# Two chained MoE layers: layer 2 of the first two blocks moved directly behind their layer 1

## The chip, the cores and the metric

The kernel runs on one core of one Trainium2 chip. The metric is the device time of one execution in microseconds. Of the kernel before three timed runs gave 1136.51, 1136.9 and 1136.9 us (median 1136.9). One further execution was profiled and took 1136.92 us.

## The reference

The input is convolved along the sequence with seven softmax-weighted taps per head (causal, zeros ahead of the start). Two dense layers follow, each in the form g(x W_in) W_out, over 8192 tokens of 192 channels with 2048 hidden columns:

```python
w = softmax(weight)                      # 8 heads x 7 taps
x = sum_k w[head, k] * x_pad[s + k]      # 2 x 4096 tokens x 192 channels
h = x @ moe_w_in                         # 192 -> 2048
g = where(h >= 1, h, where(h <= -1, 0, (h + 1) ** 2 / 4))
x = g @ moe_w_out                        # 2048 -> 192
h = x @ moe2_w_in
g = h / (1 + exp(-1.702 * h))
out = g @ moe2_w_out
```

## The kernel before

Channels lie on partitions, tokens on the free axis. The tokens are cut into 16 blocks of 512, the hidden columns of each layer into 16 slices of 128. The 192 channels of a block are a tile of 128 (a) and one of 64 (b). Every operand of a matmul is split into a high part, cast to fp32r on ACT, and a low part, the rest, subtracted on DVE (`split`, L72), and products of parts are summed in PSUM.

A unit is one slice of one layer of one block. For a unit `gemm1` makes 128 hidden rows in one of four PSUM banks (tile h), `act_a` applies the activation (layer 1: relu and square on ACT and a min on DVE, L272 to L274; layer 2: one ACT op, L276), `act_b` splits the result into ghi and glo, and `gemm2`, four units later (LAG), adds its product to the block's two accumulators. When the last slice has been added, `finish` reads the accumulators: for layer 1 into the input of layer 2 (tiles xah, xal and xb, by way of s), for layer 2 into the output.

A phase is one layer of one block: (1, 0) is layer 1 of block 0. The list `phases` (L211) and the list `units` (L219) set the order of all units by hand: blocks 0 and 1 take turns in layer 1, then block 2 goes through layer 1, then blocks 0 and 1 take turns in layer 2, and from there layer 1 of block i and layer 2 of block i - 1 alternate.

The first 32 units (WHOLE) run as whole steps: five matmuls of gemm1 and five of gemm2 over all 128 partitions (L250, L315). From there on `both` runs pairs of two units as pieces over 64 partitions, two at a time in the two halves of the array (L361). In a pair the odd unit reads the lower channels from a second copy of xb whose halves are exchanged, xc; two DMAs on SP make it (`swap_halves`, L177 to L179).

What isn't a step of a unit is put beside one: `at(step, op)` (L404) appends an operation to that step's list, and `beside` issues the list behind the step's own work. All engines take their instructions in the order in which they were issued. Three things lie there:

- Weight tiles arrive as 64-bit floats in two words. `convert_at` (L470) fetches a tile three steps ahead and turns it into a high and a low part in four steps: `begin` (an ACT op into wa, L117, and a shift on DVE into wd, L118), `join` (DVE, L122), `high_part` (a cast on ACT into wt, L127), `low_part` (two subtractions on DVE into wt, L131 and L132). A unit's gemm1 reads the low part first.
- The convolution of blocks 2j and 2j + 1 (`conv_at`, L424): seven taps on DVE for the upper channels of block 2j (cva), `put_a`, seven for the lower channels of both (cvb), and `put_b`, which splits them into xb and issues the two DMAs for xc. They begin 22 steps ahead of block 2j's layer 1, one a step. The upper channels of block 2j + 1 follow from 16 steps ahead of its own layer 1.
- The later parts of `finish` for layer 1: adding the two halves of the lower channels one step later, splitting them two steps later.

In the steady part the numbers of the first units of layer 1 of blocks 4, 6, ... 14 are 112, 176, ... 432.

Of the kernel before, what the change touches and what calls it, by code (L numbers as in the profile page):

```python
# [20 lines left out]
def kernel(  # L21
# [21 lines left out]
    nc = tc.nc  # L43
    NBLK, D, _ = out.shape
    K = taps_in.shape[2]
    NF, _, WC = w1.shape
    DB = D - P
    B = P // DB
    PAD = K - 1
    H = P // 2  # L50
    LAG = 4
    CH = 4
# [11 lines left out]
    ps = ctx.enter_context(tc.tile_pool(name="ps", bufs=1, space=bass.MemoryType.PSUM))  # L64
# [7 lines left out]
    def split(src, hi, lo):  # L72
        nc.scalar.copy(hi, src)  # L73
        nc.vector.tensor_sub(lo, src, f32(hi))  # L74
# [64 lines left out]
    def new_xs():  # L139
        return [xs_p.tile([P, T], F32R, tag=t, name=t) for t in ("xah", "xal", "xb", "xc")]  # L140
# [7 lines left out]
    def conv_taps(part, t, c):  # L148
        def tap(k):
            w, x = taps[:, part, k : k + 1], t[:, k : k + T]  # L150
            if k == 0:
                return lambda: nc.vector.tensor_scalar_mul(c, x, w)
            return lambda: nc.vector.scalar_tensor_tensor(c, x, w, c, op0=ALU.mult, op1=ALU.add)  # L153

        return [tap(k) for k in range(K)]
# [18 lines left out]
    def put_a(i, c):  # L174
        split(c, *x1[i][:2])
# [14 lines left out]
    def conv_ops(j):  # L190

        ta, tb = xt[0, B * j], xt[1, j]
        ca = cv_p.tile([P, T], F32, tag="cva", name="cva")
        cb = cv_p.tile([P, T], F32, tag="cvb", name="cvb", bufs=1)
        x1[B * j] = new_xs()
        ops = conv_taps(0, ta, ca) + [lambda: put_a(B * j, ca)]
        ops += conv_taps(1, tb, cb) + [lambda: put_b(B * j, cb)]
        st = {}

        def begin():  # L200
            st["c"] = cv_p.tile([P, T], F32, tag="cva", name="cva")
            x1[B * j + 1] = new_xs()
            st["ops"] = conv_taps(0, xt[0, B * j + 1], st["c"])
            put_b(B * j + 1, cb)

        ops.append(begin)
        ops += [lambda: st["ops"].pop(0)() for _ in range(K)] + [lambda: put_a(B * j + 1, st["c"])]
        return ops


    phases = [(1, 0), (1, 1), (1, 2), (2, 0), (2, 1)]  # L211
    for i in range(3, NBLK):
        phases += [(1, i), (2, i - 1)]
    phases += [(2, NBLK - 1)]

    def in_turn(*ps):
        return [(p, c + f) for c in range(0, NF, CH) for p in ps for f in range(CH)]

    units = in_turn(0, 1) + in_turn(2) + in_turn(3, 4)  # L219
    units += [(p, f) for p in range(5, len(phases)) for f in range(NF)]  # L220
    unit_at = {u: k for k, u in enumerate(units)}

    hid, act, halves, accs = {}, {}, {}, {}
# [145 lines left out]
    def finish(p, step):  # L369
        n, i = phases[p]  # L370
        acc_a, acc_b = accs.pop(p)
        if n == 1:
            ah, al, b, c = x2[i] = new_xs()
            s = cv_p.tile([P, T], F32, tag="cva", name="s")
            nc.scalar.copy(s[0:DB], acc_b[DB:P])
            split(acc_a, ah, al)
            at(step + 1, lambda: nc.vector.tensor_add(s[0:DB], acc_b[0:DB], s[0:DB]))  # L377

            def put():
                split(s[0:DB], b[0:DB], b[DB:P])  # L380
                if phases.index((2, i)) * NF >= WHOLE:
                    swap_halves(c, b)

            at(step + 2, put)
        else:
            o = o_p.tile([P, 2, T], F32, tag="o", name="o")
            nc.scalar.copy(o[0:DB, 1], acc_b[DB:P])
            nc.vector.tensor_add(o[0:DB, 1], acc_b[0:DB], o[0:DB, 1])
            if p < len(phases) - 1:
                nc.scalar.copy(o[:, 0], acc_a)  # L390
                nc.sync.dma_start(out[i, 0:P], o[:, 0])
                nc.sync.dma_start(out[i, P:D], o[0:DB, 1])
            else:
                near, far = slice(0, T // 2), slice(T // 2, T)
                nc.scalar.copy(o[:, 0, near], acc_a[:, near])
                nc.sync.dma_start(out[i, 0:P, near], o[:, 0, near])
                nc.scalar.copy(o[:, 0, far], acc_a[:, far])
                nc.scalar.dma_start(out[i, 0:P, far], o[:, 0, far])
                nc.sync.dma_start(out[i, P:D], o[0:DB, 1])
# [4 lines left out]
    def at(step, op):  # L404
        plan.setdefault(max(step, 0), []).append(op)

    def fetch_w(n, f):
        raw[n, f] = weight_load(n, f)
# [11 lines left out]
    def fetch_x(*which):  # L420
        for part, i in which:
            xt[part, i] = x_load(part, i)

    def conv_at(j):  # L424
        first, second = (unit_at[phases.index((1, B * j + k)), 0] for k in range(B))
        ops = []
        at(first - 30, lambda: fetch_x((0, B * j), (1, j), (0, B * j + 1)))
        at(first - 22, lambda: ops.extend(conv_ops(j)))
        for k in range(2 * (K + 1)):
            at(first - 22 + k, lambda: ops.pop(0)())  # L430
        for k in range(K + 2):
            at(second - 16 + k, lambda: ops.pop(0)())

    with tc.manual_schedule():
        nc.sync.dma_start(taps, taps_in)
        fetch_x((0, 0), (1, 0))
        fetch_w(1, 0)
        fetch_w(1, 1)
        fetch_x((0, 1))
        fetch_w(1, 2)  # L440

        make_identity(nc, ident)
        warm_up()
        softmax_taps()

        nc.scalar.activation(const.tile([P, 1], F32, name="table"), ident[:, 0:1], AF.Gelu_apprx_sigmoid)
        for i in range(B):
            x1[i] = new_xs()
        ca = cv_p.tile([P, T], F32, tag="cva", name="cva")
        cb_ps, ca_ps = bank(3, "cb_ps"), bank(2, "ca_ps")  # L450
        a0 = conv_taps(0, xt[0, 0], ca)
        b_ops = conv_on_pe(1, xt[1, 0], cb_ps, ident, nc.scalar.mul)
        a1 = conv_on_pe(0, xt[0, 1], ca_ps, ident, nc.gpsimd.tensor_scalar_mul)
        for op in b_ops:
            op()

        ws = [weight_ops(1, f, raw.pop((1, f))) for f in range(CH - 1)]
        order = a0[0:3] + ws[0][0:1] + a0[3:5] + ws[0][1:3] + a0[5:7] + ws[0][3:4] + ws[1][0:1]
        order += [lambda: put_a(0, ca)] + ws[1][1:2] + [lambda: put_b(0, cb_ps)] + ws[1][2:] + ws[2]
        for op in order:  # L460
            op()
        fetch_w(1, 3)
        for k, op in enumerate(weights_at(1, 3)):
            at(k // 2, op)
        for k, op in enumerate(a1):
            at((k + 2) // 3, op)
        at(1, lambda: put_b(1, cb_ps))
        at(2, lambda: put_a(1, ca_ps))

        def convert_at(n, f, steps):  # L470
            at(steps[0] - 3, lambda: fetch_w(n, f))
            for step, op in zip(steps, weights_at(n, f)):
                at(step, op)

        for f in range(CH, NF):
            s = f - 2 if f < 2 * CH else 2 * f - 2 * CH - 1
            convert_at(1, f, range(s, s + 4))
        for f in range(NF):
            s = 2 * NF - 2 + 4 * f if f < CH else 3 * NF - 2 + 2 * (f - CH)
            convert_at(2, f, range(s, s + 4))  # L480
        for j in range(1, NBLK // B):
            conv_at(j)

        def beside(step):
            for op in plan.get(step, []):
                op()

        def finish_if_last(u, step):
            if 0 <= u < len(units) and units[u][1] == NF - 1:
                finish(units[u][0], step)  # L490


        for step in range(WHOLE):
            gemm1(step)
            act_a(step)
            if step >= 1:
                act_b(step - 1)
            if step >= LAG:
                gemm2(step - LAG)
            finish_if_last(step - LAG - 1, step)  # L500
            beside(step)


        act_b(WHOLE - 1)
        for u in range(WHOLE, len(units) + LAG + 4, 2):
            v = u - LAG
            if u == WHOLE:
                finish_if_last(v - 1, u)
                gemm1(u)
                gemm2(v)  # L510
                gemm1(u + 1)
                gemm2(v + 1)
            elif u < len(units):
                both(u, v)
            elif v < len(units):
                gemm2(v)
                gemm2(v + 1)
            if u < len(units):
                for op in (act_a, act_b):
                    op(u)  # L520
                    op(u + 1)
            finish_if_last(v + 1, u + 1)
            for step in (u, u + 1):
                beside(step)
# [55 lines left out]
```

## Time and profile before

| | |
|---|---|
| median of the timed runs | 1136.9 us |
| profiled execution | 1136.92 us |
| its span, first to last instruction | 1135.1 us |
| busy in the span: PE, ACT, DVE | 1126.0, 824.1, 715.2 us |
| granted clock of TensorE | 0.9 or more of full speed in every slice |
| DMA | 36.69 MB, mean 32 GB/s |

All times in the rows count from the start of the span. Matmuls are pipelined and their ends are modelled, so a PE that is busy in the table need not be at its peak; idle time of PE, where it is shown in brackets behind a row with the instruction that ended it, is time in which no matmul ran. The DVE and ACT columns matter only where PE waits for them. In the span's 40 slices of 28.4 us DVE shows 7 to 9 tenths in the first five and 4 to 7 in the others, up to the last few.

### The profile page before, as it was taken

What the parts mean: (1) busy time and instruction counts of PE and PEld (TensorE: products, weight loads), DVE (VectorE), ACT (ScalarE), POOL (GpSimd) and SP (SyncE); (2) the same over time, 40 slices, a digit from 0 to 9 for tenths busy, and PEclk for the clock granted to TensorE, in tenths of its full rate; (3) what the DMA queues carried; (4) which work ended last, traced back from release to release, by engine and by line L of the source; (5) the groups of instructions that cost most, each with busy time, mean ns of one, the idle gap of its engine ahead of it and who ended that gap; (6) DMA issues with size and microseconds to landing.
All of it is one profiled execution on the core that took longest, in us unless ns stands there. A gap on an engine that the chain in (4) does not pass through costs nothing.

```text
span 1135.1 us, 23124 instructions
## 1 busy us (share of the span) xinstructions
PE 1126.0 (99%) x9468; PEld 1009.6 (89%) x9468; DVE 715.2 (63%) x1152; ACT 824.1 (73%) x1468; POOL 7.6 (1%) x13
## 2 busy tenths in 40 slices
PE   9999999999999999999999999999999999999998
PEld 5878889999999999999999999999999999999997
DVE  7997866674657756476564756647566575655532
ACT  7988976867758677686876758677586776868654
POOL 2000000000000000000000000000000000000000
PEclk9999999999999999999999999999999999999999
DMA  5312330100001000010000000010000100000000
GB/s 176 125 28 65 111 97 27 57 10 25 11 10 43 18 17 10 11 43 20 15 19 15 30 19 15 20 43 1 20 15 20 43 1 20 15 20 15 11 15 15
DMA packets 16841, 36.69 MB, mean 32 GB/s; under 512 B 2528, under 2 KB 2784, under 8 KB 16736
## 3 DMA queue, kind: packets, MB, share of 16 engines
q1 hardware_dynamic: 16592, 35.09, 10.5%
q8 instruction: 75, 1.23, 0.5%
q14 instruction: 30, 0.25, 0.1%
q10 hardware_dynamic: 144, 0.13, 0.0%
HBM read 21.05 MB, written 6.29 MB: 24 GB/s over the span
## 4 chain that ended last, share of the span: by engine, by line
PE 93%; DVE 3%; ACT 2%; issue 1%; POOL 0%; POOLq 0%; DVEq 0%
PE acc L361 47%; PE h L361 42%; PE acc L315 1%; PE h L250 1%; DVE glo L74 1%; DVE a L274 1%; ACT a L273 1%; ACT a L272 1%; PE cb_ps L170 1%; PE ca_ps L170 1%; DVE wd L122 0%; PE warm L161 0%; ACT ghi L73 0%; ACT wa L117 0%; ACT wt L127 0%
## 5 line engine op out<-in xcount | busy, mean ns | idle before, releaser
L361 PE MATMUL acc<-ghi,wt 64*128 64x512 f32 x2868 | 869.0, 386 | 0.3 <-ACT ghi L73 0.3
L361 PE MATMUL h<-xah,wt 64*128 64x512 f32 x1912 | 738.2, 386 | 0.0
L361 PE MATMUL acc<-glo,wt 64*128 64x512 f32 x1912 | 706.1, 386 | 0.1
L361 PEld LDWEIGHTS acc<-ghi,wt 64*128 64x128 f32 x2868 | 489.6, 184 | 29.8 <-ACT ghi L73 0.7
L74 DVE TENSOR_TENSOR glo<-a,ghi 128x512 fp32r<-128x512 f32 x512 | 341.6, 688 | 228.8 <-ACT ghi L73 218.6
L361 PEld LDWEIGHTS acc<-glo,wt 64*128 64x128 f32 x1912 | 351.8, 184 | 20.1 <-DVE glo L74 0.8
L361 PEld LDWEIGHTS h<-xah,wt 64*128 64x128 f32 x1912 | 351.8, 184 | 19.8 <-issue 0.4
L361 PE MATMUL h<-xal,wt 64*128 64x512 f32 x956 | 369.2, 386 | 0.0
L73 ACT CAST ghi<-a 128x512 fp32r<-128x512 f32 x512 | 301.3, 614 | 28.3 <-DVE a L274 28.1
L274 DVE SCALAR_TENSOR_TENSOR a<-h,a 128x512 f32<-128x512 f32 x256 | 176.9, 691 | 161.3 <-ACT a L273 161.2
L276 ACT ACTIVATE a<-h 128x512 f32<-128x512 f32 x256 | 151.3, 596 | 155.0 <-PE h L361 147.1
L361 PE MATMUL h<-xb,wt 64*128 64x512 f32 x717 | 238.8, 386 | 0.0
L361 PE MATMUL h<-xc,wt 64*128 64x512 f32 x717 | 238.7, 386 | 0.0
L272 ACT ACTIVATE a<-h 128x512 f32<-128x512 f32 x256 | 151.0, 590 | 53.6 <-PE h L361 53.3
L361 PEld LDWEIGHTS h<-xal,wt 64*128 64x128 f32 x956 | 175.9, 184 | 9.7
L273 ACT ACTIVATE a<-a 128x512 f32<-128x512 f32 x256 | 161.8, 632 | 8.2
L361 PEld LDWEIGHTS h<-xc,wt 64*128 64x128 f32 x717 | 131.9, 184 | 9.6
L361 PEld LDWEIGHTS h<-xb,wt 64*128 64x128 f32 x717 | 131.9, 184 | 5.0
L153 DVE SCALAR_TENSOR_TENSOR cva<-xt,taps,cva 128x512 f32<-128x512 f32 x90 | 67.3, 748 | 1.2
L153 DVE SCALAR_TENSOR_TENSOR cvb<-xt,taps,cvb 128x512 f32<-128x512 f32 x42 | 31.3, 746 | 0.4
L250 PE MATMUL h<-xah,wt 128*128 128x512 f32 x68 | 28.3, 417 | 2.6 <-DVE wt L131 2.6
L73 ACT CAST xb<-s 64x512 fp32r<-64x512 f32 x16 | 9.9, 621 | 28.2 <-DVE s L377 28.2
(61 smaller groups left out, 417.8 us busy)
## 6 DMA issues: line engine op xcount, KB each, us to landing
raw<-in_w_dram SPq DMA_DIRECT2D x32, 448.0 KB, 3.5
xc<-xb SPq DMA_DIRECT2D x46, 128.0 KB, 2.2
xt<-in_xa_dram SPq DMA_DIRECT2D x16, 259.0 KB, 3.5
out_dram<-o SPq DMA_DIRECT2D x15, 256.0 KB, 2.0
out_dram<-o SPq DMA_DIRECT2D x17, 128.0 KB, 2.3
xt<-in_xb_dram SPq DMA_DIRECT2D x8, 259.0 KB, 3.2
xb<-xc SPq DMA_DIRECT2D x14, 128.0 KB, 2.2
out_dram<-o ACTq DMA_DIRECT2D x1, 128.0 KB, 1.8
```

What stands on the lines that cost most here:

```text
L73: nc.scalar.copy(hi, src)
L74: nc.vector.tensor_sub(lo, src, f32(hi))
L153: return lambda: nc.vector.scalar_tensor_tensor(c, x, w, c, op0=ALU.mult, op1=ALU.add)
L170: return lambda: nc.tensor.matmul(c, d[:, k], t[:, k : k + T], start=k == 0, stop=k == K - 1)
L250: nc.tensor.matmul(h, w, r, start=j == 0, stop=j == len(prods) - 1)
L272: nc.scalar.activation(a, h, AF.Relu, bias=0.5, scale=0.5)
L273: nc.scalar.activation(a, a, AF.Square)
L274: nc.vector.scalar_tensor_tensor(a, h, 1.0, a, op0=ALU.max, op1=ALU.min)
L276: nc.scalar.activation(a, h, AF.Gelu_apprx_sigmoid)
L315: nc.tensor.matmul(acc, w, r, start=id(acc) in fresh, stop=last and ends[id(acc)] == k)
L361: mm = nc.tensor.matmul(banks[n], w, r, start=n in fresh, stop=ends.get(n) == k)
```

## The change

`phases` and `units` put layer 2 of blocks 0 and 1 directly behind their layer 1, in turns of 8 units, with block 2's layer 1 behind both (its first unit is 64 instead of 32). In layer 1 the turns are no longer all 4 long: block 0 ends at unit 25 instead of 27. Layer 2's weight tiles are converted from step 22 on, in place of step 30. The steps that follow the evacuation of blocks 0 and 1 (`soon`) come one or two steps sooner, and in whole steps `finish` itself comes one step sooner. The convolutions of even blocks start 18 steps ahead of their layer 1, and their fetches 28. WHOLE is unchanged.

```diff
--- before.py
+++ after.py
@@ -208,16 +208,22 @@
         return ops
 
 
-    phases = [(1, 0), (1, 1), (1, 2), (2, 0), (2, 1)]
+    phases = [(1, 0), (1, 1), (2, 0), (2, 1), (1, 2)]
     for i in range(3, NBLK):
         phases += [(1, i), (2, i - 1)]
     phases += [(2, NBLK - 1)]
 
-    def in_turn(*ps):
-        return [(p, c + f) for c in range(0, NF, CH) for p in ps for f in range(CH)]
-
-    units = in_turn(0, 1) + in_turn(2) + in_turn(3, 4)
-    units += [(p, f) for p in range(5, len(phases)) for f in range(NF)]
+    def in_turn(*runs):
+        made, us = {}, []
+        for p, n in runs:
+            f = made.get(p, 0)
+            us += [(p, f + k) for k in range(n)]
+            made[p] = f + n
+        return us
+
+    units = in_turn((0, 4), (1, 4), (0, 4), (1, 4), (0, 4), (1, 2), (0, 4), (1, 6))
+    units += in_turn((2, 8), (3, 8), (2, 8), (3, 8))
+    units += [(p, f) for p in range(4, len(phases)) for f in range(NF)]
     unit_at = {u: k for k, u in enumerate(units)}
 
     hid, act, halves, accs = {}, {}, {}, {}
@@ -374,14 +380,15 @@
             s = cv_p.tile([P, T], F32, tag="cva", name="s")
             nc.scalar.copy(s[0:DB], acc_b[DB:P])
             split(acc_a, ah, al)
-            at(step + 1, lambda: nc.vector.tensor_add(s[0:DB], acc_b[0:DB], s[0:DB]))
+            soon = i < B
+            at(step + (not soon), lambda: nc.vector.tensor_add(s[0:DB], acc_b[0:DB], s[0:DB]))
 
             def put():
                 split(s[0:DB], b[0:DB], b[DB:P])
                 if phases.index((2, i)) * NF >= WHOLE:
                     swap_halves(c, b)
 
-            at(step + 2, put)
+            at(step + (1 - i if soon else 2), put)
         else:
             o = o_p.tile([P, 2, T], F32, tag="o", name="o")
             nc.scalar.copy(o[0:DB, 1], acc_b[DB:P])
@@ -424,10 +431,10 @@
     def conv_at(j):
         first, second = (unit_at[phases.index((1, B * j + k)), 0] for k in range(B))
         ops = []
-        at(first - 30, lambda: fetch_x((0, B * j), (1, j), (0, B * j + 1)))
-        at(first - 22, lambda: ops.extend(conv_ops(j)))
+        at(first - 28, lambda: fetch_x((0, B * j), (1, j), (0, B * j + 1)))
+        at(first - 18, lambda: ops.extend(conv_ops(j)))
         for k in range(2 * (K + 1)):
-            at(first - 22 + k, lambda: ops.pop(0)())
+            at(first - 18 + k, lambda: ops.pop(0)())
         for k in range(K + 2):
             at(second - 16 + k, lambda: ops.pop(0)())
 
@@ -476,7 +483,7 @@
             s = f - 2 if f < 2 * CH else 2 * f - 2 * CH - 1
             convert_at(1, f, range(s, s + 4))
         for f in range(NF):
-            s = 2 * NF - 2 + 4 * f if f < CH else 3 * NF - 2 + 2 * (f - CH)
+            s = (22, 24, 25, 27, 28, 30, 31, 32)[f] if f < NF // 2 else 36 + (3 * f - 3 * NF // 2) // 2
             convert_at(2, f, range(s, s + 4))
         for j in range(1, NBLK // B):
             conv_at(j)
@@ -497,7 +504,7 @@
                 act_b(step - 1)
             if step >= LAG:
                 gemm2(step - LAG)
-            finish_if_last(step - LAG - 1, step)
+            finish_if_last(step - LAG, step)
             beside(step)
 
 
@@ -505,7 +512,6 @@
         for u in range(WHOLE, len(units) + LAG + 4, 2):
             v = u - LAG
             if u == WHOLE:
-                finish_if_last(v - 1, u)
                 gemm1(u)
                 gemm2(v)
                 gemm1(u + 1)
```

What this moves on the engines, at three places. First DVE near units 24 and 25, the end of layer 1's weight conversion. The number behind a tile's name is that of its allocation, but for h, where the number right behind the letter is the unit (h24 is unit 24); a row with `a<-h` is the min of that unit. Before:

```order
L274 SCALAR_TENSOR_TENSOR a_807<-h24_801,a_807 128x512
L74 TENSOR_TENSOR glo_812<-a_786,ghi_811 128x512
L131 TENSOR_TENSOR wt1_88<-wd_753,wt1_88 128x384
L132 TENSOR_TENSOR wt1_88<-wd_753,wt1_88 128x64
L153 SCALAR_TENSOR_TENSOR cvb_477<-xt_272,taps_85,cvb_477 128x512
L274 SCALAR_TENSOR_TENSOR a_829<-h25_823,a_829 128x512
L74 TENSOR_TENSOR glo_834<-a_807,ghi_833 128x512
L74 TENSOR_TENSOR xb_480<-cvb_477,xb_480 64x512
L274 SCALAR_TENSOR_TENSOR a_852<-h26_846,a_852 128x512
L74 TENSOR_TENSOR glo_857<-a_829,ghi_856 128x512
```

After:

```order
L280 SCALAR_TENSOR_TENSOR a_791<-h24_785,a_791 128x512
L74 TENSOR_TENSOR glo_796<-a_770,ghi_795 128x512
L131 TENSOR_TENSOR wt1_88<-wd_731,wt1_88 128x384
L132 TENSOR_TENSOR wt1_88<-wd_731,wt1_88 128x64
L118 TENSOR_SCALAR wd_808<-raw_734 128x448
L280 SCALAR_TENSOR_TENSOR a_819<-h25_813,a_819 128x512
L74 TENSOR_TENSOR glo_824<-a_791,ghi_823 128x512
L131 TENSOR_TENSOR wt2_89<-wd_759,wt2_89 128x384
L132 TENSOR_TENSOR wt2_89<-wd_759,wt2_89 128x64
L122 SCALAR_TENSOR_TENSOR wd_808<-wa_807,wd_808 128x448
```

In both, the low part of layer 1's last tile (L131 and L132 into wt1, from wd_753 before and wd_731 after) stands behind the min of unit 24 and the subtraction of unit 23. Before, a tap of the convolution and later the split of cvb follow; now layer 2's tiles do. The first unit that reads the tile is 27 before and 25 after.

Second ACT where block 0's layer 1 is evacuated (rows with s and xah), up to the cast of its lower channels (xb) or, before, to where that cast isn't reached yet. Before:

```order
L375 COPY s_977<-acc1_0_310 64x512
L73 CAST xah_973<-acc0_0_309 128x512
L272 ACTIVATE a_1003<-h32_981 128x512
L273 ACTIVATE a_1003<-a_1003 128x512
L272 ACTIVATE a_1007<-h33_992 128x512
L273 ACTIVATE a_1007<-a_1007 128x512
L73 CAST ghi_1011<-a_1003 128x512
```

After:

```order
L381 COPY s_941<-acc1_0_304 64x512
L73 CAST xah_937<-acc0_0_303 128x512
L127 CAST wt2_89<-wd_885 128x448
L278 ACTIVATE a_956<-h30_950 128x512
L279 ACTIVATE a_956<-a_956 128x512
L73 CAST ghi_960<-a_924 128x512
L127 CAST wt2_89<-wd_913 128x448
L117 ACTIVATE wa_972<-raw_888 128x448
L73 CAST xb_939<-s_941 64x512
L278 ACTIVATE a_986<-h31_980 128x512
```

Before, the units behind the evacuation are those of block 2's layer 1 (h32 and h33), and the cast of xb comes behind two more of them. Now it stands between units 30 and 31, with two copies and a first op of layer 2's tiles ahead of it, and unit 32 is the first that reads xb.

Third ACT ahead of layer 1 of block 4, whose first unit is 112, in the steady part; a row `xb<-cvb` is the cast of the convolution's lower channels. Before:

```order
L276 ACTIVATE a_3321<-h104_3277 128x512
L276 ACTIVATE a_3323<-h105_3278 128x512
L73 CAST ghi_3325<-a_3321 128x512
L73 CAST ghi_3329<-a_3323 128x512
L73 CAST xb_2903<-cvb_2900 64x512
L276 ACTIVATE a_3382<-h106_3338 128x512
L276 ACTIVATE a_3384<-h107_3339 128x512
L73 CAST ghi_3386<-a_3382 128x512
L73 CAST ghi_3390<-a_3384 128x512
L276 ACTIVATE a_3438<-h108_3394 128x512
L276 ACTIVATE a_3440<-h109_3395 128x512
```

After:

```order
L73 CAST ghi_3445<-a_3441 128x512
L73 CAST ghi_3449<-a_3443 128x512
L73 CAST xb_3031<-cvb_3028 64x512
L282 ACTIVATE a_3502<-h110_3458 128x512
L282 ACTIVATE a_3504<-h111_3459 128x512
L73 CAST ghi_3506<-a_3502 128x512
L73 CAST ghi_3510<-a_3504 128x512
L278 ACTIVATE a_3558<-h112_3514 128x512
L279 ACTIVATE a_3558<-a_3558 128x512
L278 ACTIVATE a_3562<-h113_3515 128x512
L279 ACTIVATE a_3562<-a_3562 128x512
```

The cast stood behind unit 105, with three pairs between it and unit 112. It now stands behind unit 109, with one pair between them. DVE's subtraction and the two DMAs for xc follow it in both.

## Rows read from the trace of the kernel before

**Rows 1.** Windows by stage: stretch, its length, busy us (instructions) of each engine.

```profile
core 0: us, PE busy (x) PEld busy (x) DVE busy (x) ACT busy (x) POOL busy (x), PEclk, DMA share, GB/s
...
44.40:79.30 34.90, 32.27 (x142) 25.87 (x140) 34.84 (x70) 30.45 (x56) 0.00 (x0) 1.00 0.13 40
...
118.20:1121.60 1003.40, 1003.40 (x8856) 914.95 (x8854) 609.72 (x952) 718.31 (x1273) 0.00 (x0) 1.00 0.08 24
...
```

**Rows 2.** Timeline of PE, pairs: start, duration, instruction, idle before and releaser.

```profile
112.75 0.39 PE L361 MATMUL h<-xah,wt 64*128 64x512 f32 x1
113.44 0.50 PE L361 MATMUL acc<-ghi,wt 64*128 64x512 f32 x1 [0.31 <-ACT ghi L73]
...
113.78 0.39 PE L361 MATMUL acc<-ghi,wt 64*128 64x512 f32 x1
...
118.16 0.39 PE L361 MATMUL h<-xah,wt 64*128 64x512 f32 x1
...
264.60 0.39 PE L361 MATMUL h<-xah,wt 64*128 64x512 f32 x1
...
266.42 0.39 PE L361 MATMUL h<-xc,wt 64*128 64x512 f32 x1
```

**Rows 3.** Timeline of PE, first matmuls of whole units 5, 18, 19, 27, 28.

```profile
26.15 0.39 PE L250 MATMUL h<-xah,wt 128*128 128x512 f32 x1
...
55.62 0.39 PE L250 MATMUL h<-xah,wt 128*128 128x512 f32 x1
...
59.07 0.50 PE L250 MATMUL h<-xah,wt 128*128 128x512 f32 x1 [1.03 <-DVE wt L131]
...
79.26 0.50 PE L250 MATMUL h<-xah,wt 128*128 128x512 f32 x1 [1.60 <-DVE wt L131]
...
81.67 0.39 PE L250 MATMUL h<-xah,wt 128*128 128x512 f32 x1
```

**Rows 4.** Timeline of ACT, tile conversions without taps (first five) and with them.

```profile
40.23 0.62 ACT L117 ACTIVATE wa<-raw 128x448 f32<-128x448 f32 x1
40.76 0.57 ACT L272 ACTIVATE a<-h 128x512 f32<-128x512 f32 x1
...
42.41 0.59 ACT L272 ACTIVATE a<-h 128x512 f32<-128x512 f32 x1
...
44.49 0.57 ACT L127 CAST wt<-wd 128x448 fp32r<-128x448 f32 x1 [0.32 <-DVE wd L122]
44.96 0.61 ACT L117 ACTIVATE wa<-raw 128x448 f32<-128x448 f32 x1
...
55.03 0.61 ACT L117 ACTIVATE wa<-raw 128x448 f32<-128x448 f32 x1
...
60.20 0.61 ACT L117 ACTIVATE wa<-raw 128x448 f32<-128x448 f32 x1
```

**Rows 5.** Timeline of DVE, low parts of tiles 8 and 15 of layer 1.

```profile
43.23 0.55 DVE L131 TENSOR_TENSOR wt<-wd,wt 128x384 fp32r<-128x384 f32 x1
...
78.65 0.55 DVE L131 TENSOR_TENSOR wt<-wd,wt 128x384 fp32r<-128x384 f32 x1
```

**Rows 6.** Timeline of all engines: evacuation on ACT, then the lower channels' split.

```profile
102.72 0.58 ACT L375 COPY s<-acc 64x512 f32<-64x512 f32 x1
...
103.80 0.61 ACT L117 ACTIVATE wa<-raw 128x448 f32<-128x448 f32 x1
...
109.95 0.62 ACT L73 CAST xb<-s 64x512 fp32r<-64x512 f32 x1 [0.88 <-DVE s L377]
...
110.61 0.69 DVE L74 TENSOR_TENSOR xb<-s,xb 64x512 fp32r<-64x512 f32 x1
```

**Rows 7.** Timeline of SP: issues of the copies xc, block 4's and block 14's.

```profile
256.61 0.46 SPq L178 DMA_DIRECT2D xc<-xb  x1
257.17 0.55 SPq L179 DMA_DIRECT2D xc<-xb  x1
...
945.68 0.46 SPq L178 DMA_DIRECT2D xc<-xb  x1
```

**Rows 8.** Waits of SP, 250 to 260 us: us in total, times, longest.

```profile
SPq L178 <- DVE xb L74: 6.8, 1, 6.8
```

**Rows 9.** Tile xc, 248 to 258 us: its DMAs from issue to landing.

```profile
DMA to landing us min/median/max: 2.2/2.2/2.3
```

**Rows 10.** Page, costliest groups: busy, mean ns of one, idle before.

```profile
L153 DVE SCALAR_TENSOR_TENSOR cva<-xt,taps,cva 128x512 f32<-128x512 f32 x90 | 67.3, 748 | 1.2
```

## The prediction

> **What bounds the kernel now.** Read the page first: its slices show a TensorE that is busy nearly all the time and the clock granted in full. Then the windows by stage say where the exceptions are. Between 118.2 and 1121.6 us PE has no idle time at all [rows 1]; there the kernel is a row of paired steps, each 4.307 us: (264.60 - 118.16) / 34 pairs [rows 2]. So nothing that the change does there can gain; it can only add waits, and every wait of PE there moves the end by its whole length. Ahead of it, from 44.4 to 79.3 us, DVE is busy 34.84 of 34.90 us [rows 1]. PE steps there take (55.62 - 26.15) / 13 = 2.267 us each, and PE loses time twice, both times to the DVE subtraction that ends a weight tile (line 131) [rows 3].
>
> What the start loses now: unit 28 would begin at 26.15 + 23 x 2.267 = 78.29 and begins at 81.67, so 3.4 us, the restart of 0.14 us after a wait included (81.67 - 79.26 = 2.41 instead of 2.267) [rows 3]. The pair that begins at 112.75 lasts to 118.16, 5.41 us instead of 4.31, held at its second pair of matmuls by an ACT cast [rows 2]: 1.1 us. Together 4.5 us, which is all that the change could ever win.
>
> **The change, part by part.** The sum is made against the profiled execution, 1136.92 us (span 1135.1 and 1.8 outside it), which is the median of the timed runs too. The number of units, matmuls, casts, taps and DMAs is the same in both kernels; only places move.
>
> (a) Taps leave steps 10 to 26, and layer 1's last tiles are wanted sooner. With taps of block 2 in the way, one weight tile takes 60.20 - 55.03 = 5.17 us of two steps; just before the first tap it took 44.96 - 40.23 = 4.73 us [rows 4]. That period isn't the work of one engine (ACT alone has 2 x 1.65 + 0.53 + 0.47 = 4.3 us) but a ring: square on ACT, then on DVE the min, the low half of the activation, the tile's low half and the next tile's join, then on ACT the tile's copy, the next tile's first op, the next unit's relu and square. I take 4.73 for steps without taps. It is still more than PE's 2 x 2.267 = 4.53, so the ring falls behind by 0.2 us per tile instead of 0.64. Tile 8's low half starts at 43.23 in both kernels [rows 5]. Tile 15's is seven periods later: 43.23 + 7 x 4.73 = 76.34, where it is 78.65 now [rows 5]: 2.3 us sooner. But the uneven turns want it at unit 25 instead of 27, 4.53 us sooner. PE starts 0.61 us after that subtraction starts (79.26 - 78.65), so at 76.95; on time it would be 26.15 + 20 x 2.267 = 71.49. Late by 5.46, with restart 5.6 us, against 3.4 now: **+2.2 us**, PE waiting at units 24 and 25. From below: -3.4, if the ring goes at PE's rate once taps are gone. From above: the tile of layer 2 that now begins in step 22 adds a join and a first op just there; if the last three tiles go at 5.17 again, 1.3 more, +3.5.
>
> (b) Block 0's output of layer 1 is now wanted three steps after its evacuation (step 29, unit 32), where it was sixteen (step 32, unit 48), and tiles of layer 2 are converted in those steps. From unit 25 PE needs 7 steps: unit 32 at 76.95 + 0.14 + 15.87 = 92.96, and its fourth matmul, which reads the lower 64 channels, 0.68 later, 93.6. ACT can begin unit 25's relu when its five matmuls end, 76.95 + 0.14 + 1.3 = 78.4 (five of ten matmuls, 1.13, and 0.16 that the last one's duration of 0.39 exceeds its share [rows 3]). From there to the cast of those channels ACT has six units at 1.65, four first ops at 0.53, four copies at 0.47 [rows 4] and the two evacuations, 103.80 - 102.72 = 1.08 [rows 6]: 15.0 us, so 93.4. The cast and the subtraction behind it end 0.66 + 0.69 later (109.95 to 110.61, and the duration of the latter [rows 6]): 94.75. PE waits 1.15, with restart **+1.3 us**. Nothing covers it: every PE instruction behind unit 32 waits too. Between 0 (if unit 25 is late for another reason, ACT has idled less) and 3.9 (if these four tiles go by the ring, 4 x 4.73 = 18.9 instead of 15.0).
>
> (c) The 1.1 us at 112.75 came from layer 1 units of block 2 beside the evacuations of blocks 0 and 1 and two tiles. Now units 34 to 42 are layer 2, with one ACT op where layer 1 has two. I count **-1.1 us**; tiles 6 and 7 are then wanted two pairs after their conversion, so a new wait as long as the old one is the upper bound (0).
>
> (d) The convolution of each even block starts 18 steps before its layer 1, where it was 22. The last of its sixteen operations casts and subtracts the lower channels, and then two DMAs on SP copy them with halves exchanged (lines 178, 179); each odd unit's pieces read that copy (xc). Count it from the first such place in the steady part: SP issues line 178 at 256.61, as soon as DVE has written xb, which is what that queue waits for [rows 7, 8], and the DMA lands 2.2 us later [rows 9]: 258.81. The phase that reads it begins at 264.60, the first read of xc is at 266.42 [rows 2], so it now has 7.6 us to spare. Moved by four steps, two pairs, the copy comes 8.61 us later against its reader: it is **late by 1.0 us**, and matmuls leave PE in order, so all of PE waits. The issue repeats to 0.01 us: 945.68 is 5 x 137.81 after 256.61 [rows 7], and 137.81 is 32 pairs. Blocks 2, 4, ... 14 make seven such places, the first now at unit 65. After a wait inside a pair the next matmul starts 0.34 instead of 0.23 later (113.44 to 113.78 [rows 2]), so 1.1 each: **7 x 1.1 = +7.7 us**. From below 0, if some slack that rows don't show lets the copy go earlier. From above: were the read to wait for the second half as well (issued 0.56 later, at 257.17, landing by 259.5 with the longest 2.3 [rows 7, 9]), 1.66 and 0.1 each, +12.3. I take the first, as the matmul reads only the half that the first DMA writes. The odd blocks' second convolution keeps its place.
>
> The Trainium skill (DMA: Bandwidth & Descriptors, Rules for kernel authors) says to issue a DMA early and wait for it late, since its fixed cost then overlaps; the change goes against it, as only 1.2 us of compute are left between the issue and the reader. The same page (Anatomy of one DMA) prices a transfer at 2.0 us plus its bytes over 436 GB/s, for the path from GpSimd: 2.3 us for 128 KB, an estimate by that page, where the row has 2.2. By it each place would cost 0.1 more and the sum would be 0.7 higher.
>
> Weight fetches keep three steps of lead, and the swaps of blocks 0 and 1 have over 1 us to spare by the same count as in (d); I cost both at nothing. Evacuating one step sooner is inside (b).
>
> Sum: 2.2 + 1.3 - 1.1 + 7.7 = +10.1 us, 1136.9 + 10.1 = **1147.0 us**.
>
> **Rivals.**
> 1. The taps alone decide. DVE is the full engine before 79.3 us, its taps go, and without the two taps of a period (at most 0.75 each [rows 10]) its 5.17 us come to some 3.7, which fits in PE's 4.53; if tiles then come at PE's rate, all 4.5 us of waits vanish, and if the copy comes in time too, 1136.9 - 4.5 = 1132.4 us: faster. Against it: the ring's 4.73 was measured where no tap ran, and the 1.0 us of (d) is a difference of times that repeat exactly. It decides if tile 15 is ready before 71.5 us. Chance 0.06.
> 2. As forecast at the start, but the copy is not late: +2.4, 1139.3 us. For it: 1.0 us is less than half of one landing. Chance 0.06, half of which I count as no change, since +2.4 is just the 0.2% (2.3 us) that a measurement can tell here.
> 3. The start wins its 4.5 us and the copies cost 7.7: +3.2, 1140.1 us. Chance 0.08.
> 4. The reader waits for both halves: +2.4 + 12.3, 1151.6 us. Against it: separate reads of the two halves, and separate DMAs. Chance 0.06.
>
> **How the numbers follow.** The forecast itself has 0.74; its own range is 1142 to 1151, by (a) and (b) between their ends. To leave out no more than 2 in 10 the low end goes to rival 3: 1140 to 1151. Faster is rival 1, 0.06; within 0.2% half of rival 2 and the edge of rival 3, 0.04; slower the rest, 0.90.
>
> **What would show it.** (d): in the changed profile PE has seven idle gaps of about 1 us, 64 units apart from the second on, each ended by a DMA that writes xc, and the stretch from about 120 us on is no longer without idle time. (a): PE waits for line 131 at units 24 and 25, some 2 us each, and tile periods on ACT between 45 and 70 us are 4.73. (b): a wait of about 1 us at unit 32 for the subtraction that writes xb. (c): no wait of PE for an ACT cast near unit 42. I am wrong if the steady stretch stays free of idle time, or if tiles come at 4.53 us or less.

## The result, and the profile after

The changed kernel takes 1149.8 us (median of 4 runs, 1149.17 to 1150.74) against 1136.8 for the kernel before: ratio 1.0115, 95% interval 1.0098 to 1.0133. It is slower, by 13.0 us; forecast were 10.1 more. The profiled run of the changed kernel took 1149.17 us, span 1147.4, so profile against profile 12.3 us have to be found.

The page says first what did not change: 9468 matmuls, and the same DVE and ACT operations but for their places. New is the idle time in its line on the reads of xc. Columns: busy us, mean ns of one, idle us before it, releaser:

```profile
L367 PE MATMUL h<-xc,wt 64*128 64x512 f32 x717 | 239.5, 387 | 5.8 <-DMA xc<-xb 5.8
```

The steady stretch, which was without idle time before [rows 1], now has 1012.00 - 1006.23 = 5.8 us of it, all of it in that line (busy us and instructions of each engine, granted clock, DMA share, GB/s):

```profile
core 0: us, PE busy (x) PEld busy (x) DVE busy (x) ACT busy (x) POOL busy (x), PEclk, DMA share, GB/s
122.00:1134.00 1012.00, 1006.23 (x8860) 841.07 (x8858) 616.45 (x946) 718.73 (x1268) 0.00 (x0) 1.00 0.07 20
```

PE's timeline of the changed kernel has every wait that the prediction speaks of. In brackets stand the idle time before the matmul and what ended it:

```profile
72.67 0.50 PE L256 MATMUL h<-xah,wt 128*128 128x512 f32 x1 [2.17 <-DVE wt L131]
...
77.75 0.49 PE L256 MATMUL h<-xah,wt 128*128 128x512 f32 x1 [1.00 <-DVE wt L131]
...
80.16 0.39 PE L256 MATMUL h<-xah,wt 128*128 128x512 f32 x1
...
93.76 0.39 PE L256 MATMUL h<-xah,wt 128*128 128x512 f32 x1
...
96.30 0.73 PE L256 MATMUL h<-xb,wt 128*128 128x512 f32 x2 [1.69 <-DVE xb L74]
...
98.02 0.39 PE L256 MATMUL h<-xah,wt 128*128 128x512 f32 x1
...
168.12 0.50 PE L367 MATMUL h<-xc,wt 64*128 64x512 f32 x1 [0.64 <-DMA xc<-xb]
...
273.32 0.50 PE L367 MATMUL h<-xc,wt 64*128 64x512 f32 x1 [1.24 <-DMA xc<-xb]
...
412.12 0.50 PE L367 MATMUL h<-xc,wt 64*128 64x512 f32 x1 [0.70 <-DMA xc<-xb]
...
550.97 0.49 PE L367 MATMUL h<-xc,wt 64*128 64x512 f32 x1 [0.73 <-DMA xc<-xb]
```

Units 24 and 25 wait for the low part of layer 1's last two weight tiles, unit 32 for the lower channels of block 0's output, and seven pairs (the last three at 689.79, 828.59 and 967.80) for the copy xc.

The account, in us of one profile against the other. "Before" of each row is worked out in the same way from [rows 2, 3].

| Stretch | Working | More than before | Forecast |
|---|---|---|---|
| up to unit 5 | starts at 26.59, was 26.15; ahead of every row that the change moves | +0.4 | 0 |
| (a) to the end of unit 25 | 80.16 - (26.59 + 21 x 2.267) = 6.0 lost, was 3.4 | +2.6 | +2.2 |
| (b) unit 32 | 98.02 - 93.76 - 2.267 | +2.0 | +1.3 |
| (c) units 33 to 43 | 98.02 to 122.34 is 24.3; was 25.2 (93.00 to 118.16) | -0.8 | -1.1 |
| (d) the rest | 1147.4 - 122.34 = 1025.1; was 1016.9 | +8.1 | +7.7 |

The sum is +12.3, and what lies outside the span is 1.8 us in both.

### The profile page after: what moved, and what is told of

It reads as the page before. It is cut to its first block, busy times and chain, and to the rows that moved or that the text cites. A ratio compares the mean times of both kernels' runs of the same rounds, so it can differ in the third digit from the quotient of the medians.

```text
span 1147.4 us, 23139 instructions
## 1 busy us (share of the span) xinstructions
PE 1129.9 (98%) x9468; PEld 937.3 (82%) x9468; DVE 717.0 (62%) x1152; ACT 825.1 (72%) x1468; POOL 6.7 (1%) x13
## 3 DMA queue, kind: packets, MB, share of 16 engines
HBM read 21.05 MB, written 6.29 MB: 24 GB/s over the span
## 4 chain that ended last, share of the span: by engine, by line
PE 91%; ACT 3%; DVE 3%; DMA 2%; issue 1%; SPq 0%; DVEq 0%
PE acc L367 47%; PE h L367 42%; DMA xc<-xb 1%; PE h L256 1%; PE acc L321 1%; DVE glo L74 1%; ACT a L279 1%; ACT a L278 1%; DVE wd L122 1%; PE ca_ps L170 1%; ACT wt L127 1%; ACT wa L117 0%; DVE wt L131 0%; DMA raw<-in_w_dram 0%; ACT ghi L73 0%
## 5 line engine op out<-in xcount | busy, mean ns | idle before, releaser
L367 PE MATMUL acc<-ghi,wt 64*128 64x512 f32 x2868 | 913.4, 386 | 0.0
L367 PE MATMUL acc<-glo,wt 64*128 64x512 f32 x1912 | 736.3, 386 | 0.0
L367 PEld LDWEIGHTS acc<-ghi,wt 64*128 64x128 f32 x2868 | 524.4, 184 | 51.9
L321 PE MATMUL acc<-ghi,wt 128*128 128x512 f32 x102 | 29.6, 398 | 0.0
```

What stands on the lines that cost most here:

```text
L321: nc.tensor.matmul(acc, w, r, start=id(acc) in fresh, stop=last and ends[id(acc)] == k)
L367: mm = nc.tensor.matmul(banks[n], w, r, start=n in fresh, stop=ends.get(n) == k)
```

## The experiments

**The copies alone.** The changed kernel with the even blocks' convolutions back at 22 steps, their fetches at 30:

```diff
-        at(first - 28, lambda: fetch_x(...))
-        at(first - 18, lambda: ops.extend(conv_ops(j)))
+        at(first - 30, lambda: fetch_x(...))
+        at(first - 22, lambda: ops.extend(conv_ops(j)))
...
-            at(first - 18 + k, lambda: ops.pop(0)())
+            at(first - 22 + k, lambda: ops.pop(0)())
```

> The changed kernel with its convolutions 22 steps ahead again (fetches 30), all else as changed. Theory: the seven waits for the copy xc were 8.1 of the 12.3 us that the profiled run lost; with 7.6 us of slack they all go, and what is left is the start: 1149.8 - 8.1 = 1141.7 us, no idle time of PE behind 125 us. Rival A (the taps' later place costs time in itself, by what they displace on DVE and ACT): waits for xc go, others take their place, 1146 or more. Rival B (the start is the larger part): under 2 us are won.

Measured: 1140.83 us (5 runs), ratio to before 1.0033 (1.0021 to 1.0046). So 1149.8 - 1140.8 = 9.0 us, over two thirds of the loss, hang on this one number. PE's steady stretch is full again, with the clock unchanged:

```profile
122.00:1126.00 1004.00, 1004.00 (x8859) 846.84 (x8858) 615.15 (x947) 716.45 (x1267) 0.00 (x0) 1.00 0.07 20
```

The waits at units 24, 25 (2.12 and 2.01) and 32 (1.69) stayed, and with them 3.8 us of loss. That of unit 25 is longer here than in the changed kernel (1.00); the reason is TensorE's clock, see (a) below.

**The same number put into the kernel before**, with everything else as it was: 30 becomes 28, 22 becomes 18, in the lines above.

> The kernel before with its convolutions 18 steps ahead (fetches 28), old order of units. Theory: six places wait for xc (blocks 4 to 14) at 1.15 us each, +6.9; block 2's lies in the whole steps, where its taps come 4 steps later, so tile 11 is no longer late and tile 15 about half a us sooner, -1.5: 1136.9 + 5.4 = 1142.3 us. Rival A (the lateness of the copies depends on the new order of units): no waits for xc, 1135 to 1137. Rival B (lateness is partly given back behind each place): under 1140.

**And for block 2 alone**, whose copy no pair waits for:

```diff
+        ahead = 18 if j == 1 else 22
-        at(first - 30, lambda: fetch_x(...))
-        at(first - 22, lambda: ops.extend(conv_ops(j)))
+        at(first - ahead - 8, lambda: fetch_x(...))
+        at(first - ahead, lambda: ops.extend(conv_ops(j)))
...
-            at(first - 22 + k, lambda: ops.pop(0)())
+            at(first - ahead + k, lambda: ops.pop(0)())
```

> The kernel before with block 2's convolution alone 18 steps ahead (fetch 28), the others 22. Theory: no wait for xc anywhere; tile 11 of layer 1 comes 1.0 us sooner (ring period 4.73 for four steps more), so PE's wait at unit 19 falls from 1.2 to about 0.2; tile 15 comes 0.5 us sooner against a PE that is 1.0 earlier, so that wait stays near 1.5 to 2: 1136.9 - 1.4 = 1135.5 us. Rival: DVE's backlog is the same by tile 15 wherever the taps stand in steps 10 to 29, the end of the stage doesn't move: 1136.7 to 1137.0.

Measured: 1143.19 us (ratio 1.0053, 1.0037 to 1.0068) for the first, 1136.12 (0.9992, 0.9983 to 1.0000) for the second. The two kernels differ in six places where a pair reads the copy, and 7.07 / 6 = 1.18 us is what one costs, without any of the new order of units. The first of the six, in the trace of the kernel with all convolutions at 18:

```profile
267.40 0.50 PE L361 MATMUL h<-xc,wt 64*128 64x512 f32 x1 [1.06 <-DMA xc<-xb]
```

The next four wait 0.69 to 0.73 and the last 1.39. Block 2's own move loses the wait at unit 19 but not the one at unit 27, which is as long as before [rows 3]:

```profile
78.00 0.50 PE L250 MATMUL h<-xah,wt 128*128 128x512 f32 x1 [1.60 <-DVE wt L131]
```

0.9 us are gained, against 1.4 expected, at the edge of what a measurement can tell.

**Two steps further**, to see whether a place costs what the count of pairs says: the changed kernel with 18 made 16 and 28 made 26.

> The changed kernel with its convolutions 16 steps ahead (fetches 26), one pair later still. Theory: the copies come 4.31 us later against their readers, which wait for all of it, one for one and seven times: 1149.8 + 7 x 4.31 = 1180 us, seven idle gaps of PE of about 5.2 us (xb itself, made in the pair just ahead, may take over as the one waited for, at much the same time). Rival (a wait is partly given back, or the copies are issued by another event than the split): under 1165.

Measured, in a single run: 1193.81 us. (1193.8 - 1140.8) / 7 = 7.6 us a place, where 1.2 and one more pair's length should have given 5.5. There are two waits a place: seven for ACT's cast of xb, and behind each one for the copy (totals in us, times, longest):

```profile
PE h L367 <- ACT xb L73: 22.1, 7, 3.2
...
PE h L367 <- DMA xc<-xb: 7.7, 7, 2.4
```

That is (22.1 + 7.7) / 7 = 4.3 a place, less than the 5.2 expected. What the time has above that is for the most part the clock. Windows around one such place (a wait of 3.15 us ends at 426.15, a second of 0.44 at 429.09):

```profile
424.00:426.00 2.00, 0.00 (x0) 0.00 (x0) 1.45 (x3) 0.52 (x1) 0.00 (x0) 0.79 0.00 0
426.00:428.00 2.00, 1.85 (x8) 1.50 (x10) 0.69 (x1) 0.10 (x1) 0.00 (x0) 0.50 0.00 1
428.00:430.00 2.00, 1.56 (x8) 0.81 (x6) 0.00 (x0) 0.00 (x0) 0.00 (x0) 0.50 0.57 130
430.00:432.00 2.00, 2.00 (x12) 1.51 (x12) 0.00 (x0) 0.00 (x0) 0.00 (x0) 0.51 0.00 0
432.00:434.00 2.00, 2.00 (x22) 1.63 (x20) 0.61 (x1) 1.85 (x4) 0.00 (x0) 1.00 0.00 0
```

From 426 to 432 us PE is granted 0.50, which is 1.2 of 2.4 GHz. By the timeline 10 matmuls start in the 2 us from 430 to 432 and 18 in the next 2 (the counts in the rows include those begun before): 0.9 us lost with no wait at all. So the places lost more than their waits, and the expectation, which had only the waits, was too low.

**The ring** (the run that later expectations call e5). The prediction took the 4.73 us of a weight tile for a cycle that passes from ACT to DVE and back. If so, it becomes shorter when the cycle is cut, with the same work on both engines. In layer 1's last eight tiles, `begin` and `join` (and with them the fetch) come one step sooner than the copy's step asks:

```diff
-            convert_at(1, f, range(s, s + 4))
+            convert_at(1, f, range(s, s + 4) if f < 2 * CH else (s - 1, s, s + 2, s + 3))
```

> The changed kernel, layer 1's tiles from 8 on begun one step earlier and their high part cast two steps behind the join instead of one; low part where it was. Theory (the period of 4.73 us is a ring from DVE's join over ACT's copy back to the next min): the copy no longer waits for the join of the step just gone, tiles follow PE at 4.53 us or less, PE's wait at unit 24 goes and that at unit 25 is about 2 us (its tile's low part stands only one step ahead): the 6.0 us lost there fall to some 2.5, 1149.8 - 3.5 = 1146.3 us. Rival (ACT's own work is the limit: 4.3 of 4.53 us and small waits): tiles stay at 4.73, 1149 to 1150.

Measured: 1147.14 us (ratio 1.0085, 1.0071 to 1.0099), 2.7 less than the changed kernel. DVE's low parts of two successive tiles are now 4.31 us apart, which is ACT's work for a tile as the prediction summed it (4.3); ACT is busy for 24.62 of the 25 us from 45 to 70:

```profile
47.38 0.55 DVE L131 TENSOR_TENSOR wt<-wd,wt 128x384 fp32r<-128x384 f32 x1
...
51.69 0.55 DVE L131 TENSOR_TENSOR wt<-wd,wt 128x384 fp32r<-128x384 f32 x1
```

The wait at unit 24 is gone, that at unit 25 is 1.98; unit 32 waits 1.69 as before. Of the 3.5 us expected 0.8 are missing. In its profile TensorE's clock falls behind the wait of 1.98: units 25 and 26 take 6.29 us (74.09 to 80.38), where the kernel with all three edits, below, takes 4.71 at full clock.

**What the two gains make together.** The kernel before, with block 2's convolution at 18 and the ring cut, so both edits above in one kernel:

```diff
+        ahead = 18 if j == 1 else 22
...
+            convert_at(1, f, range(s, s + 4) if f < 2 * CH else (s - 1, s, s + 2, s + 3))
```

> The kernel before with block 2's convolution 18 steps ahead and the same two moves of tile pieces as in e5. Theory: up to step 14 tiles follow PE; from there to step 26 DVE's own work (5.17 us per two steps with two taps) sets the period, 0.64 more than PE, five tiles: the wait at unit 27 falls from 2.0 to under 1, 1136.1 - 1 = 1135.1 us. Rival (with taps DVE is full either way and the moves change nothing): 1136.1.

Measured: 1134.30 us (11 runs), ratio 0.9981 (0.9972 to 0.9990). It beats both kernels, if by 0.2% only. Unit 27 waits next to nothing:

```profile
76.21 0.50 PE L250 MATMUL h<-xah,wt 128*128 128x512 f32 x1 [0.26 <-DVE wt L131]
```

**Unit 32.** The split of the lower channels (`put`) one step sooner for block 0, so in the step of the evacuation, where block 1's is already, in the changed kernel with convolutions at 22:

```diff
-            at(step + (1 - i if soon else 2), put)
+            at(step + (0 if soon else 2), put)
```

> The changed kernel with convolutions 22 ahead and only block 0's lower channels split in the step of their evacuation. Theory (unit 32 waits for xb because a copy, a first op and unit 30 stand ahead of its cast on ACT): the cast starts at about 93.4 instead of 94.6 (the sum of the two halves on DVE ends then), DVE's subtraction follows at once, the wait of 1.7 us falls to 0.2: 1140.8 - 1.5 = 1139.3 us. Rival (the sum on DVE is what is late; ACT only waits for it): 1140.5 or more, as unit 30's relu is now held up behind it.

Measured: 1141.14 us (ratio 1.0035, 1.0023 to 1.0047), no better than the 1140.83 without it. The wait did go, and came back elsewhere. Its PE timeline:

```profile
94.98 0.72 PE L256 MATMUL h<-xb,wt 128*128 128x512 f32 x2 [0.25 <-DVE xb L74]
...
101.42 0.49 PE L367 MATMUL acc<-glo,wt 64*128 64x512 f32 x1 [0.69 <-DVE glo L74]
```

and ACT's:

```profile
93.59 0.62 ACT L73 CAST xb<-s 64x512 fp32r<-64x512 f32 x1 [1.42 <-DVE s L384]
```

Unit 33 starts 1.8 us sooner than without the edit (96.70 against 98.50, 0.4 of it from the start-up), unit 42 only 0.6 (117.88 against 118.52). ACT now stands idle for 1.42 us in front of the cast, for the sum on DVE, and the units behind it are later with their low parts: that of unit 31, which PE waits for at 101.42, starts on DVE at 100.69 instead of 99.53. Here, where ACT is short of time, the work behind the moved operation is late in its place.

**All three edits in the changed kernel:** convolutions at 22, the ring cut, the split sooner.

> The changed kernel with convolutions 22 ahead, tile pieces as in e5, and block 0's lower channels split in the step of their evacuation. If the three terms add: 1140.8 - 3.5 - 1.5 = 1135.8 us, ahead of the kernel before (1137.0). Rival: with the waits at 24 and 25 gone ACT has less time in hand, and xb is waited for by what was won: 1139 or more.

Measured: 1138.24 us (11 runs, 1136.64 to 1139.39), ratio 1.0009 (1.0000 to 1.0018). It lies between the 1135.8 of a plain sum and the 1139 of the rival. In its profile (a run of 1136.64) the wait for the low part of an activation at the first pairs is there again, 0.71 us at 96.83. Its runs fall into two groups, and TensorE's mean granted clock parts them: four at 1136.64 to 1136.87 us with 1.000, seven at 1138.11 to 1139.39 with 0.998. The size fits a fall of the clock at unit 25. The profiled run waits 2.01 us there, keeps 1.00, and needs 4.71 us for units 25 and 26 (73.26 to 77.97), 1.6 less than the kernel with the ring cut alone after its fall. That the seven lost their time at this place is not shown, as none of them was profiled, and what makes the clock fall in one execution and not in the next stays open.

## Why the prediction was right

**(d), the late copy: right in cause, place and count.** Seven waits, at the first odd unit of blocks 2, 4, ... 14, each ended by the DMA. The changed kernel's queue at the first place:

```profile
165.90 0.47 SPq L178 DMA_DIRECT2D xc<-xb  x1
166.42 0.59 SPq L179 DMA_DIRECT2D xc<-xb  x1
```

165.90 plus a landing of 2.2 [rows 9] is 168.10, and the read starts at 168.12. The second half, issued at 166.42, can't have landed by then, so rival 4, in which the reader waits for both, is out by the trace. A regular place costs (689.79 - 550.97) - 137.81 = 1.0 us over the 32 pairs' length, just short of the 1.1 forecast. Five of the seven cost that or little less; the others cost more, because the landing is not always 2.2. At the place that waits 1.24, DMAs into xc took

```profile
DMA to landing us min/median/max: 2.7/2.9/3.1
```

and at the one that waits 1.07 they took 2.6 to 2.9. The prediction took the landing from one place and used it for seven.

The idle time in brackets is not the whole cost. It counts from the modelled end of the matmul before, 0.39 after its start where 0.23 is the usual distance, and the next matmul starts 0.34 behind the read instead of 0.23: 0.16 + 0.11 more a place, 5.8 + 7 x 0.27 = 7.7 in all. That this is the forecast to the tenth is in part luck, since short places and two longer landings cancel. Of the 0.4 left in the account's 8.1, 0.3 is not the copies': in the kernel with the convolutions at 22 the same stretch has no wait and is 1140.0 - 122.83 = 1017.2 us long, against 1016.9 before. By the medians of the runs the copies cost 9.0; 0.6 of the difference is the changed kernel's median over its profiled run, and the clock at units 24 to 26, see (a), differs between executions too.

**(a), the ring: right, undersized by 0.4, which is the clock.** The tiles come at 4.73 on both engines in the changed kernel, ACT:

```profile
45.41 0.61 ACT L117 ACTIVATE wa<-raw 128x448 f32<-128x448 f32 x1
...
50.14 0.62 ACT L117 ACTIVATE wa<-raw 128x448 f32<-128x448 f32 x1
```

and DVE, six periods of 4.73 from tile 8 to tile 14 and one of 5.09 to tile 15:

```profile
43.68 0.55 DVE L131 TENSOR_TENSOR wt<-wd,wt 128x384 fp32r<-128x384 f32 x1
...
72.06 0.55 DVE L131 TENSOR_TENSOR wt<-wd,wt 128x384 fp32r<-128x384 f32 x1
...
77.15 0.55 DVE L131 TENSOR_TENSOR wt<-wd,wt 128x384 fp32r<-128x384 f32 x1
```

Cutting the cycle took the period to 4.31, so it is one. This is also what refutes rival 1, which had the taps alone decide: without a tap the tiles still came slower than PE's 4.53. The 0.4 comes by way of TensorE's clock, which the prediction left out. After the wait of 2.17 us it is at half for most of unit 24. Windows of the changed kernel (columns as above; the granted clock is the third number from the end):

```profile
70.00:72.00 2.00, 0.50 (x3) 0.07 (x1) 1.21 (x3) 1.97 (x5) 0.00 (x0) 1.00 0.41 113
72.00:74.00 2.00, 1.33 (x5) 1.06 (x6) 2.00 (x6) 1.93 (x4) 0.00 (x0) 0.84 0.29 117
74.00:76.00 2.00, 2.00 (x6) 1.63 (x5) 1.38 (x4) 1.32 (x3) 0.00 (x0) 0.50 0.67 192
76.00:78.00 2.00, 0.99 (x3) 0.27 (x3) 2.00 (x5) 1.39 (x3) 0.00 (x0) 0.81 0.10 38
```

Unit 24's matmuls come 0.43 apart there instead of 0.23. Tile 15's low part stands on DVE behind the min of unit 24, so the slow matmuls reach it through ACT, on the changed kernel's timeline:

```profile
74.65 0.60 ACT L278 ACTIVATE a<-h 128x512 f32<-128x512 f32 x1 [0.69 <-PE h L256]
...
75.94 0.69 DVE L280 SCALAR_TENSOR_TENSOR a<-h,a 128x512 f32<-128x512 f32 x1 [0.62 <-ACT a L279]
```

ACT stands idle for unit 24's matmuls, DVE then for ACT, and two operations behind the min the tile is 5.09 - 4.73 = 0.36 late.

The kernel with the convolutions at 22 has the same instructions up to step 34, and its trace shows this stretch at full clock. In its profiled run unit 24 waits 2.12 us, the clock stays at 1.00, and tile 15 comes 4.57 behind tile 14, not 5.09:

```profile
72.00:74.00 2.00, 1.97 (x9) 1.63 (x10) 2.00 (x5) 1.83 (x4) 0.00 (x0) 1.00 0.05 5
...
71.43 0.55 DVE L131 TENSOR_TENSOR wt<-wd,wt 128x384 fp32r<-128x384 f32 x1
...
76.00 0.55 DVE L131 TENSOR_TENSOR wt<-wd,wt 128x384 fp32r<-128x384 f32 x1
...
76.61 0.50 PE L256 MATMUL h<-xah,wt 128*128 128x512 f32 x1 [2.01 <-DVE wt L131]
```

Unit 25 starts there 76.61 - 25.98 = 50.6 us behind unit 5, which is the forecast's 76.95 - 26.15 = 50.8, and waits the "some 2 us" that the prediction named. Only behind this second wait does the clock fall, and units 25 and 26 take 6.29 us instead of 4.71. So the ring itself was sized right, and the term left out, the clock, cost 0.5 in the changed kernel's profile (51.2 us from unit 5 to unit 25 instead of 50.6) and 1.6 in this one.

**(b), unit 32: right in place and releaser, undersized (1.3 for 2.0).** The subtraction that unit 32 needs was put to end at 94.75 and ends at 96.25, on the changed kernel's ACT and DVE:

```profile
94.60 0.60 ACT L73 CAST xb<-s 64x512 fp32r<-64x512 f32 x1
...
95.56 0.69 DVE L74 TENSOR_TENSOR xb<-s,xb 64x512 fp32r<-64x512 f32 x1
```

Of these 1.5 us, 0.8 is the later start (unit 32 at 93.76, not 92.96), which moves unit 32 too and costs nothing there. The rest is the miss: 0.4 in ACT's stretch, counted as work alone (cast at 94.60, where 93.4 and the 0.8 make 94.2), and 0.3 on DVE, which is busy without a gap with a tile's parts when the cast ends. The upper bound, all four tiles by the ring, was far off the other way. That this wait can't be had out by moving the split alone, the run with the sooner split showed.

**(c): right in sign,** 0.8 for 1.1. At unit 38 the first matmul starts 0.38 behind the one before it instead of 0.23; the trace names nothing that it waited for. This 0.15 us is the only sign of the new wait that was the upper bound.

The start-up's 0.4 lies ahead of everything changed, and it is spread between executions: with the old order of units unit 5 starts at 26.15, 26.65, 25.77 and 25.92 us in the four traces, with the new one between 25.55 and 26.59.

Rivals 2 and 3 fall with (d) and (a): the copy is late wherever it comes at 18 steps, in both kernels, and the start does not win its 4.5 us. What the new order was worth in itself: with the convolutions at 22 it is 3.8 us slower than the kernel before, 2.6 + 2.0 - 0.8 by the account above, so it lost at the start too.

## What to carry to other kernels

Where an engine is full, find the slack of each transfer that it reads, from the end of the producing instruction to the first read, and compare it with every step by which something is moved: here 7.6 us of slack less 8.6 of move was the larger part of the result, and could be read before. A copy that is late by little is late every time, so multiply by the places; take its landing from several places, not one. When two in-order engines hand work back and forth, measure the period of the cycle instead of each engine's sum, and look for the hand-over that can be made a step sooner.

## What the runs showed of the hardware

A wait of TensorE can cost more than its length. After the waits of 3.15 us in the kernel with convolutions at 16, the granted clock was 0.50 for about 6 us, and a place cost 7.6 us for 4.3 of waits; after 2.17 us at unit 24 it was at 0.50 from 74 to 76 us and back in full only after 76. After the waits of 0.64 to 1.24 us at the copies, the steady stretch as a whole stayed at 1.00. The length alone does not decide it: behind 2.12 us (unit 24, convolutions at 22) and 2.01 us (unit 25, all three edits) the clock stayed at 1.00, behind 1.98 us (unit 25, ring cut) it fell. How long and how idle PE must have been for it was not measured.

The same 128 KB copy on SP's queue landed in 2.2 us at most places, and in 2.6 to 3.2 at two of seven in the changed kernel and at two of six, the first and the last, in the kernel before with convolutions at 18. At the first such place in the changed kernel, the issue behind it took 1.39 instead of 0.59:

```profile
271.08 1.39 SPq L179 DMA_DIRECT2D xc<-xb  x1
```

The profile shows one thing more at these places, a transfer of 0.02 MB on a queue that it lists as q8, of kind instruction. From 269 to 275 us of the changed kernel:

```profile
q1 hardware_dynamic: 160, 0.26, 18.9%
q8 instruction: 1, 0.02, 1.2%
```

From 408.5 to 414.5 us, where the copy landed in 2.2, the profile has no row for q8. Of the 30 pairs of copies between xb and xc in the changed kernel six have such a transfer while they are under way, and these six have median landings of 2.6 to 3.7 us; the other 24 have 2.2 or 2.3. No run moved these transfers, so that they are what slows the copies is not shown.
